# Identity products on TensorE beside a decode kernel's attention: the last kept unit and the twelve V's of a row's chain

## The chip, the cores and the metric

The kernel runs on one core of one Trainium2 chip. The metric is the device time of one execution in microseconds. The engines are named as in the profile: PE (TensorE's matmuls), PEld (its weight loads), DVE (VectorE), ACT (ScalarE), POOL (GpSimd) and SP (SyncE, which issues nearly all transfers).

## The reference

Two layers of attention over a long cache, each followed by a small MLP, run one after the other on the same row vector `x`; both use the same caches and weights. Eight batch rows, one token each, 16 query heads of 256 on 8 key/value heads, 4096 cached positions, model width 448, hidden width 1792.

```python
def _A_ref(x, k_cache, v_cache, wq, wo):          # x (8, 1, 448); caches (8, 8, 4096, 256), bf16
    q = (x @ wq).reshape(B, 1, 16, 256).transpose(0, 2, 1, 3)
    k, v = (jnp.repeat(c, 2, axis=1) for c in (k_cache, v_cache))
    p = softmax(einsum("bhqd,bhkd->bhqk", q, k) * 256 ** -0.5)
    o = einsum("bhqk,bhkd->bhqd", p, v)
    return o.transpose(0, 2, 1, 3).reshape(B, 1, 4096) @ wo

x = x + _A_ref(_layernorm(x), ...)
x = x + _B_ref(_layernorm(x), ...)
x = x + _A_ref(_layernorm(x), ...)
x = x + _B_ref(_layernorm(x), ...)
```

With one token per row the shifts in `_B_ref` push the mixing branch out of the window, so it comes to `x + gelu(layernorm(x) @ w3) @ w4`. The caches are 268 MB; the kernel reads them nearly twice, once for each layer, except for the parts that it keeps on the chip.

## The kernel before

**Units.** The work is cut into units (pass, row, gp): the pass is the first or second attention layer, gp is one of four pairs of key/value heads. A unit has four K chunks and four V chunks of 1 MB (128 partitions by 4096 bf16). `items` is the static order of all chunks; one loop walks over it (L1320 to the end of `layers_unshifted`), and each turn ends with `emit_loads`, which puts as many transfers into SP's queue as there are free places. There are 17 places of 1 MB in SBUF (`NC`, `places_t`).

**Kept units.** For each row the pairs `keep = [2, 3]` are loaded once: 14 of their 16 chunks stay in places from the first pass to the row's second pass, and two more are put away in PSUM banks (`away`, `part_words`, `inner_words`). So for each row the order is: the units of gp 2 and 3 in the first pass, with other units among them (`first_kept`); then the V's of the units that went ahead, which need the few places that are left; then gp 3 and gp 2 in the second pass from the kept places, which frees these for the loads of what follows.

**The chain.** When the V's of the last kept unit (0, row, gp 3) are done, the row's first attention layer is complete, and everything up to its second query can be worked out: the output projection, the MLP with its norms, and the projection of the new query (`chain`: `kept_half`, `mlp`, `project_q`; then `give_q`, which spreads the query with L439 on PE and L445 on DVE). This is a Python generator; `step` runs it from one `yield` to the next. Its pieces are put between the V's of three other units: twelve V chunks, each loaded as two halves (`halved`, L975). These twelve are `narrow`. For them `pv` (L1133) takes its 16 matmuls as two times eight and calls `between` in the middle, so that a piece of the chain can run after each half; the first of the twelve (`begins`) has no `between`. Ten of the twelve stand ahead of the row's second pass, two among its first scores.

**What PE runs.** `scores` (L1065) multiplies 8-column weights from the query with K, 256 columns at a time, in four column groups of the array; `pv` (L1133) does the same with the probabilities and V. `transpose_p` (L1116) turns the probabilities into `misc`, ACT copies them to `psv` (L1123). `wide` (L201) is the chain's product for one row: 128x128 weights and a vector that is read 32 times over, so 32 columns. In fp32 stand the sum of the norm (L290), the softmax sums (L562) and the scaling of a finished output (L630).

**Shared PSUM.** `misc` is one PSUM bank. Columns 0 to 127 belong to `transpose_p`; the chain's small results lie in the others, and DVE and ACT read them. PE runs its instructions in the order of the program, and a matmul into `misc` waits until the reads that the program holds it against are done.

**Queues.** All transfers of K, V and weights stand in SP's one queue, in the order of `items`. A K of the second pass's new units is loaded as a pair of 2 MB (L958) when two adjacent places are free; the halves of a `narrow` V (L975) when the half before has been multiplied out of its place.

The few lines that the edit touches in the loop are these (the condition of `between` and what follows `pv`):

```python
                pv(
                    o_now, slot, c, gp, ring_of[it],
                    (lambda: step(idx, True)) if it in narrow and it not in begins else None,
                    rest_t if halfway(it) else None,
                    it in fresh,
                )
                if ps == 0 and inside(it):
                    away(inner_words(slot))
```

Of the kernel before, what the change touches and what calls it, by code (L numbers as in the profile page):

```python
# [40 lines left out]
def layers_unshifted(  # L41
# [156 lines left out]
    def wide(out, w, x, start, stop):  # L198

        wide_done[0] += 1  # L200
        nc.tensor.matmul(  # L201
            bass.AP(out.tensor, out.offset, [out.ap[0], (1, WIDE)]),
            w,
            x.to_broadcast([128, WIDE]),
            start=start,
            stop=stop,
            skip_group_check=True,
        )

    def xbs(nb):  # L210
        return xb[1] if nb == 1 else xb[Bn][:, :, :nb]
# [913 lines left out]
    def pv(o_ps, v, a, gp, r, between, v2=None, fresh=False):  # L1125

        g = 2 * gp + a // 2
        for y in range(16):
            if y == 8 and between is not None:
                between()  # L1130
            q = y % 4
            at = 128 * r + 8 * (4 * q + y // 4) + 6 - 2 * (g % 4)
            nc.tensor.matmul(  # L1133
                o_ps[32 * q : 32 * q + 8, :],
                ptz[:, at : at + 8],
                v[:, y * Dh : (y + 1) * Dh]
                if v2 is None or y < PR
                else v2[:, (y - PR) * Dh : (y - PR + 1) * Dh],
                start=fresh and y < 4,
                stop=(y >= 12),  # L1140
                skip_group_check=True,
            )
# [177 lines left out]
    for idx, it in enumerate(items):  # L1320
# [80 lines left out]
        elif kv == 0:  # L1401
            if (ps, b) not in state:
                if ps == 1:
                    while (1, b) not in state:
                        step(10 * len(items), True, ("chain",))
                else:
                    state[0, b] = {}
            st = state[ps, b]
            who = q_key(ps, b, gp)
            if who not in q_of:  # L1410
                give_q(who)
            qbd = qbds[q_of.index(who)]
            if "z" not in st:
                z_t = chn.tile([128, 2, GP], FP32, tag="zall", bufs=8)
                st["z"] = z_t
                if final:
                    st["y"] = store[2][:, 0 : 4 * (Bn - MID)].rearrange("p (f b) -> p f b", f=4)
                    oc = store[3][:, 0 : 2 * Hq].rearrange("p (j h) -> p j h", j=2)
            if not kept_now:
                transpose_k(slot, late(it) and c % 2 == 0)  # L1420
            if c == 3 and q_begun:
                run(q_begun.pop())
            if not alone:
                step(idx)
            x = c - c % 2
            scored = not paired(n, c) or c % 2 == int(late(it))
            turn = turn_p if scored and p_of and n not in p_of else None
            if not paired(n, c):
                scores(p, c, qbd, gp, between=turn)
            elif scored:  # L1430
                two = [
                    where[(b, gp), (0, k)] if kept_now else where[n, 0, k] for k in (x, x + 1)
                ]
                if abs(two[1] - two[0]) == 1:
                    scores(two[0], x, qbd, gp, also=two[1], between=turn)
                else:
                    scores(two[0], x, qbd, gp, between=turn)
                    scores(two[1], x + 1, qbd, gp)
            if c == 1:
                p_n = work.tile([128, 4, 32, 4], BF16, tag="p_sb", bufs=1)  # L1440
                p_of[n] = p_n
            if c == 2:
                q_ahead(idx)
            if c % 2 == 1:
                exps(p_of[n], st["z"], gp, c // 2)
                if kept_now and c == 3:
                    alone.clear()
        else:
            st = state[ps, b]
            if ps == 1 and (halfway(it) or inside(it)):  # L1450
                while moves and any(w.offset == v.offset for _, w in moves for _, v in (part_words if halfway(it) else inner_words)(slot)):
                    move()
            if it in narrow and it[2] == 0 and not alone and any(e["kind"] == "chain" for e in gens):
                alone.append(n)
            if n in p_of:
                turn_p()
            spread_p(it)
            if it in v_next:
                spread_p(v_next[it])
            if final and gp in free and c == 1:  # L1460
                rz_gp = run(z_cols(st["z"], [gp]))
            if it not in narrow:
                step(idx)
            if final and gp in free:
                pv_cols(oc, slot, c, gp, psv[slot_of[n]])
                if c % 2 == 1:

                    u = c // 2
                    scale_o(oc, rz_gp, gp, u, OT2[:, :, :, b])
                    h0 = 8 * gp + 4 * u  # L1470
                    while any(e["kind"] == "last" for e in gens):
                        step(10 * len(items))
                    run(
                        add_cols(
                            st["y"],
                            lambda i: OT2[:, i % 2, i // 2, MID:],
                            lambda i, at: wo_of(i, at, end_wo),
                            range(h0, h0 + 4),
                            4,
                            open=(claim(st), gp == free[-1] and u == 1),  # L1480
                        )
                    )
            else:
                g8 = gp // 2
                alone_now = (ps, b) in split and gp in free
                if it == v_first[n] and ("o", g8) not in st:
                    while not free_o:
                        if not locked and not out_sb and waiting and waiting[0]["done"]():
                            empty(waiting[0])
                            clear(waiting.pop(0))  # L1490
                        else:
                            step(10 * len(items))
                    st["o", g8] = free_o.pop(0)
                    fresh.add(it)
                if it == v_first[n]:
                    o_of[n] = st["o", g8]
                o_now = o_of[n]
                kept_2 = (ps, gp) == (0, keep[0])
                if it == v_first[n] and (
                    alone_now or kept_2 or pairs_done.get((ps, b), 0) % 2 == 1  # L1500
                ):
                    done = pairs_done.get((ps, b), 0) + 1

                    def ready(k=(ps, b), done=done):
                        return pairs_done.get(k, 0) >= done

                    if ps == 0 and done == 4:
                        add_gen("chain", chain(b, st, ready), main=True)
                    elif kept_2:
                        rec = {"ps": st.pop(("o", 1))}  # L1510
                        add_gen("chain", kept_half(b, st, gp, ready, rec, 4))
                    elif ps == 1 and done == 2:
                        add_gen("chain" if final else "last", first_last(b, st, ready))
                    else:
                        rec = {"ps": st.pop(("o", 0)), "done": ready}
                        waiting.append(rec)
                        gps = [gp] if alone_now else free
                        if ps == 0:
                            add_gen("chain", first_half(b, st, gps, ready, rec))
                        else:  # L1520
                            add_gen("last", last(b, st, gps, ready, rec))
                pv(
                    o_now,
                    slot,
                    c,
                    gp,
                    ring_of[it],
                    (lambda: step(idx, True)) if it in narrow and it not in begins else None,
                    rest_t if halfway(it) else None,
                    it in fresh,  # L1530
                )
                if ps == 0 and inside(it):
                    away(inner_words(slot))
                if ps == 0 and halfway(it):
                    away(part_words(slot))
            if it == v_last[n]:
                pairs_done[ps, b] = pairs_done.get((ps, b), 0) + 1
                free_slots.append(slot_of.pop(n))
# [367 lines left out]
```

## Time and profile before

| | |
|---|---|
| median of 3 runs | 1033.46 us (1033.12 to 1033.53) |
| the profiled execution | 1034.17 us, of it the span 1032.5 us |
| instructions | 28801; PE 12708 matmuls and as many weight loads |
| busy | PE 658.4 us (64%), PEld 416.9 (40%), DVE 585.8 (57%), ACT 213.1 (21%), POOL 35.3 (3%) |
| granted TensorE clock, mean | 0.618 |
| transfers | 421.54 MB, mean 408 GB/s |
| matmuls, mean and count | L1133 382 ns x3808; L1065 384 ns x3456 with 256 columns, 274 ns x1280 with 128; L201 181 to 190 ns x2016; fp32 318 to 361 ns |

The span is the time from the first to the last instruction; the profiled execution's own time has a little more around it. The granted clock is the share of TensorE's pulses that its throttle let through. In the timeline a matmul's length holds its way through the array too, so that matmuls overlap: the pace is read from the distance of their starts. "idle before <-releaser" is the time that the engine sat idle and what ended it. The chain of work that ended last goes to 55% through transfers, to 20% through PE and to 18% through DVE.

### The profile page before, as it was taken

The numbers are of one execution on the slowest core, as the hardware profiler recorded it, in microseconds if no ns is written. First come the engines' busy times: TensorE is split into PE (matmuls) and PEld (weight loads), VectorE is DVE, ScalarE is ACT, GpSimd is POOL, SyncE is SP. The second block draws the span as 40 slices with busy tenths as digits, with TensorE's granted clock in tenths as the row PEclk, the third lists the DMA queues.
The fourth block names the chain that finished last, engine by engine and source line by source line (L and its number), as shares of the span: only waits on it lengthen the run. The fifth ranks groups of instructions, "written<-read, shape, count | busy, mean of one in ns | idle before, by whom it ended". The sixth has DMA issues, their size and how long they took to land.

```text
span 1032.5 us, 28801 instructions
## 1 busy us (share of the span) xinstructions
PE 658.4 (64%) x12708; PEld 416.9 (40%) x12708; DVE 585.8 (57%) x1213; ACT 213.1 (21%) x689; POOL 35.3 (3%) x138
## 2 busy tenths in 40 slices
PE   2153545876578658765775687557765775677675
PEld 2032323453245335532553355334533453345444
DVE  6345576259615961696159615971596159625672
ACT  1010111141204121412141204120412141204020
POOL 0000000000000000000000000000000000000000
PEclk9965555565656565755665657566656565667655
DMA  9999999999999999999999999999999999999994
GB/s 374 411 428 421 422 425 417 401 423 425 412 399 425 425 412 400 417 424 414 400 420 426 414 394 421 424 415 404 417 422 411 404 416 427 414 396 411 419 418 183
DMA packets 68016, 421.54 MB, mean 408 GB/s; under 512 B 7080, under 2 KB 11952, under 8 KB 42288
## 3 DMA queue, kind: packets, MB, share of 16 engines
q1 hardware_dynamic: 67840, 419.66, 99.0%
q8 instruction: 100, 1.64, 0.6%
q14 instruction: 28, 0.23, 0.1%
q10 hardware_dynamic: 48, 0.01, 0.0%
HBM read 419.63 MB, written 0.01 MB: 406 GB/s over the span
## 4 chain that ended last, share of the span: by engine, by line
DMA 55%; PE 20%; DVE 18%; issue 3%; ACT 2%; SPq 1%; POOL 0%; DVEq 0%; ACTq 0%
DMA places<-in_A_v_cache_dram 37%; DMA places<-in_A_k_cache_dram 17%; DVE places L1050 14%; PE sc L1065 8%; PE o L1133 5%; PE misc L630 2%; PE misc L201 2%; DMA w_sb<-in_B_w_dram 1%; DVE qbd L445 1%; ACT p_n L1074 1%; SPq L220 1%; DVE store L1096 1%; PE misc L562 1%; PE misc L483 0%; PE misc L1116 0%
## 5 line engine op out<-in xcount | busy, mean ns | idle before, releaser
L1050 DVE STREAM_TRANSPOSE places<-places 128x512 uint32<-128x512 uint32 (+2 forms) x384 | 443.9, 1212 | 43.9 <-DMA places<-in_A_k_cache_dram 43.6
L1133 PE MATMUL o<-places,ptw 128*8 128x256 bf16 x3808 | 246.7, 382 | 142.1 <-DMA places<-in_A_v_cache_dram 113.1
L1065 PE MATMUL sc<-places,qbd 128*8 128x256 bf16 (+1 forms) x4736 | 234.7, 354 | 147.7 <-DVE places L1050 145.8
L1065 PEld LDWEIGHTS <-qbd 128*8 128x8 bf16 x4736 | 122.5, 105 | 214.7 <-DVE places L1050 124.1
L1133 PEld LDWEIGHTS <-ptw 128*8 128x8 bf16 x3968 | 103.3, 102 | 208.8 <-issue 131.0
L1074 ACT ACTIVATE p_n<-sc 128x256 bf16<-128x256 f32 x128 | 95.5, 746 | 328.4 <-PE sc L1065 326.3
L1315 ACT COPY ptw<-psv 128x32 bf16<-128x32 bf16 x248 | 52.6, 227 | 179.5 <-PE o L1133 177.9
L445 DVE CAST qbd<-misc 32x16 bf16<-32x16 f32 (+1 forms) x184 | 30.8, 167 | 63.8 <-PE misc L439 61.9
L630 PE MATMUL misc<-R_t,o_t 128*128 128x4 f32 (+1 forms) x212 | 45.6, 322 | 27.3 <-DVE qbd L445 11.0
L630 PEld LDWEIGHTS misc<-R_t,o_t 128*128 128x128 f32 x212 | 41.4, 272 | 44.0 <-issue 17.2
L1123 ACT CAST psv<-misc 128x128 bf16<-128x128 f32 x64 | 17.0, 266 | 194.6 <-PE misc L1116 191.6
L565 DVE RECIPROCAL rz<-misc 128x4 f32<-128x4 f32 (+1 forms) x55 | 9.5, 172 | 82.8 <-PE misc L562 37.6
L1101 ACT COPY places<-store 128x1024 bf16<-128x1024 bf16 x40 | 40.2, 1027 | 10.5 <-PE o L1133 10.1
L562 PE MATMUL misc<-zm,few 128*128 128x4 f32 (+1 forms) x110 | 28.0, 325 | 18.9 <-DVE zm L554 16.5
L570 POOL TENSOR_TENSOR seen<-seen,rz 128x4 f32<-128x4 f32 (+1 forms) x55 | 11.0, 200 | 840.2 <-DVE rz L565 840.2
L562 PEld LDWEIGHTS misc<-zm,few 128*128 128x128 f32 x110 | 23.2, 262 | 35.0 <-DVE zm L554 23.3
L201 PEld LDWEIGHTS <-w_sb 128*128 128x128 bf16 x896 | 27.3, 104 | 16.1 <-issue 16.1
L1074 ACT ACTIVATION_READ_ACCUMULATOR p_n<-sc 128x1 f32 x128 | 33.8, 264 | 0.0
L584 ACT COPY o_t<-o 128x256 f32<-128x256 f32 x53 | 19.8, 373 | 58.9 <-PE o L1133 58.9
L1096 DVE TENSOR_SCALAR store<-places 128x512 uint32<-128x512 uint32 x40 | 24.8, 673 | 0.0
L634 DVE CAST qT<-misc 128x8 bf16<-128x8 f32 (+1 forms) x37 | 7.2, 196 | 28.8 <-PE misc L630 20.8
L1116 PEld LDWEIGHTS <-p_n 128*128 128x128 bf16 x256 | 11.5, 104 | 29.6 <-issue 18.5
(165 smaller groups left out, 393.1 us busy)
## 6 DMA issues: line engine op xcount, KB each, us to landing
places<-in_A_k_cache_dram SPq DMA_DIRECT2D x79, 2048.0 KB, 15.3
places<-in_A_v_cache_dram SPq DMA_DIRECT2D x193, 512.0 KB, 7.2
places<-in_A_v_cache_dram SPq DMA_DIRECT2D x87, 1024.0 KB, 19.2
places<-in_A_k_cache_dram SPq DMA_DIRECT2D x34, 1024.0 KB, 12.0
rest<-in_A_v_cache_dram SPq DMA_DIRECT2D x8, 640.0 KB, 16.7
places<-in_A_wq_dram SPq DMA_DIRECT2D x5, 768.0 KB, 12.7
places<-in_A_v_cache_dram SPq DMA_DIRECT2D x8, 384.0 KB, 16.3
wo_sb<-in_A_wo_dram SPq DMA_DIRECT2D x1, 2688.0 KB, 19.0
```

The lines of the kernel that those rows point to most:

```text
L201: nc.tensor.matmul(bass.AP(out.tensor, out.offset, [out.ap[0], (1, WIDE)]), w, x.to_broadcast([128, WIDE]), start=start, stop=stop, skip_g ...
L445: nc.vector.tensor_copy(qbd[32 * a : 32 * a + 32, :, g0 : g0 + ng, a, :], qs.rearrange("p e (f g u h) -> p (e f) u g h", f=2, u=2, h=2)[:, ...
L562: nc.tensor.matmul(z_ps, ones, zm[:], start=True, stop=True)
L584: nc.scalar.copy(o_t[:], rec["ps"])
L630: nc.tensor.matmul(ot_ps[:, j], o_sb[:].rearrange("p (i j) -> p j i", j=2)[:, j], R, start=True, stop=True)
L1050: nc.vector.transpose(w, w)
L1065: nc.tensor.matmul(sc[32 * k : 32 * k + 8, 128 * (x % 2) : 128 * (x % 2 + nx)], qbd[:, ep, gp % 2].rearrange("p a h -> p (a h)"), v, start ...
L1074: nc.scalar.activation(p_sb[:, :, :, 2 * u : 2 * u + 2].rearrange("p t i x -> p x t i"), sc[:, 0:256].rearrange("p (x t i) -> p x t i", x= ...
L1096: nc.vector.tensor_single_scalar(kept_words.bitcast(U32), words.bitcast(U32), 0, op=ALU.bitwise_or)
L1101: nc.scalar.copy(words, kept_words.bitcast(BF16))
L1133: nc.tensor.matmul(o_ps[32 * q : 32 * q + 8, :], ptz[:, at : at + 8], v[:, y * Dh : (y + 1) * Dh] if v2 is None or y < PR else v2[:, (y - ...
L1315: nc.scalar.copy(ptw[:, ring_of[it], :, 6:8], psv[slot_of[it[0]]][:, it[2]])
```

## The change

A function `fill(n)` issues n matmuls of the bf16 identity (128x128, as weights and as moving operand, 128 columns) into columns 0 to 127 of `misc`. Nobody reads what they write: `transpose_p` overwrites it. They are issued at four spots: after each K chunk and after each V chunk of the last kept unit of the first pass (ten each time), and in the middle and at the end of each `narrow` V (three each time; in the middle only where `between` is given).

```diff
+    def fill(n):
+
+        for _ in range(n):
+            nc.tensor.matmul(misc[:, 0:128], identb[:], identb[:], start=True, stop=True)
...
         for y in range(16):
             if y == 8 and between is not None:
+                fill(3)
                 between()
...
                     scores(two[0], x, qbd, gp, between=turn)
                     scores(two[1], x + 1, qbd, gp)
+            if (ps, gp) == (0, keep[1]):
+                fill(10)
             if c == 1:
...
                     rest_t if halfway(it) else None,
                     it in fresh,
                 )
+                if it in narrow:
+                    fill(3)
+                elif (ps, gp) == (0, keep[1]):
+                    fill(10)
                 if ps == 0 and inside(it):
```

On PE this adds 1192 matmuls and 1192 weight loads: in each of the eight rows 80 for the kept unit and 69 for the twelve V's. The order of all other instructions is as before on every engine. Eleven of the added matmuls in a row, the last row one fewer, wait for DVE or ACT to have read `misc`.

## The prediction

> **What bounds the kernel now.** I read the page's slices first, then stretches of one row's chain, then the order of instructions on PE inside them.
>
> ```profile
> PE   2153545876578658765775687557765775677675
> DVE  6345576259615961696159615971596159625672
> PEclk9965555565656565755665657566656565667655
> DMA  9999999999999999999999999999999999999994
> GB/s 374 411 428 421 422 425 417 401 423 425 412 399 425 425 412 400 417 424 414 400 420 426 414 394 421 424 415 404 417 422 411 404 416 427 414 396 411 419 418 183
> ```
>
> The DMA engines are busy from end to end: 421.5 MB at some 410 GB/s are the span of 1032.5 us. What can still be won are the dips to about 400 GB/s, one per batch row (eight, every fourth slice). In those slices PE is at its busiest (7 or 8 tenths) and DVE at its idlest: these are the chains. The granted clock stays near half there.
>
> ```profile
> 595.00:604.00 9.00, 8.10 (x149) 4.96 (x149) 1.95 (x12) 0.66 (x3) 0.70 (x1) 0.50 0.97 362
> 604.00:618.00 14.00, 10.72 (x218) 6.50 (x221) 3.21 (x18) 1.47 (x7) 0.55 (x1) 0.50 1.03 413
> 606.40:609.80 3.40, 3.31 (x73) 2.22 (x69) 0.66 (x4) 0.22 (x1) 0.00 (x0) 0.50 1.03 418
> 616.60:620.00 3.40, 2.72 (x52) 1.63 (x48) 0.00 (x0) 0.18 (x1) 0.00 (x0) 0.50 1.04 408
> 620.00:623.40 3.40, 2.21 (x58) 1.47 (x53) 0.98 (x6) 1.33 (x5) 0.00 (x0) 0.99 1.05 413
> ```
>
> Columns: stretch and its length, busy time of PE, PEld, DVE, ACT, POOL, then clock, DMA share, GB/s. One row's chain begins badly (362 GB/s for 9 us) and then runs at 413. Against 412 the eight beginnings lose 0.54, 0.49, 0.13, 0.26, 1.09, 0.21, 0.02 and 0.81 us (stretches of 5 to 9 us at 380, 383, 401, 394, 362, 395, 410, 345), and the eight starts of the second pass 0.29, 0.34, 0.54, 0.39, 0.05, 0.36, 0.20 and 0.60 us. Together 6.3 us (two of the stretches overlap a little): no more can be won.
>
> The third and fourth lines show what moves the clock. PE is busy for 3.31 of 3.40 us and the clock stays at half; it is busy for 2.72 us and the next stretch has the full clock. The records of the clock change only in steps of 3.413 us, that is 4096 columns at half clock (below). I counted the columns that the matmuls stream in each step, an 8-wide one (L1065, L1133) as a quarter, for four of them run abreast: 606.4 has 0.65 of 4096, 616.6 has 0.75. Of the half-clock steps from 50 us on, all 31 with over 0.74 are followed by a full one, 5 of 10 between 0.70 and 0.74, none of 190 below. A full step is kept by 17 of 17 over 0.70 and by 1 of 38 below.
>
> **The change part by part.** It adds 1192 matmuls of 128x128 by 128 columns and as many weight loads to PE and nothing to other engines: per row 8 bursts of ten in the unit gp 3, and 23 bursts of three in the twelve V's.
>
> *Price of one.* The trace has no such matmul. Its matmuls with 32 columns at L201 start 27 ns apart at half clock, 25 at full; an 8-wide one with 256 columns has its share of four abreast in 53 and 27 ns. So 128 columns take 107 ns at half clock (4 x 27), and at full between 53 (the same columns at twice the rate) and 100 (4 x 25, were those bound by columns). I take 53, for the columns of L1133 do halve: three cost 0.32 or 0.16 us, ten 1.07 or 0.53. The Trainium skill (TensorE: Matmul & The Clock Gate, Back-to-back issue gap) gives about 81 ns a matmul for a sustained stream of weight loads and matmuls of 128 columns; by that three cost 0.24 us and the sums below for the full clock rise by half. A burst between two V halves also changes weights twice where none did before: a half (8 matmuls, 0.43 us) has L201 0.53 us after it, and L201 x20 (0.54) is followed 0.74 us on, so 0.10 and 0.20 us; beside an L201 step nothing is added.
>
> *The tens.* Four bursts stand beside the unit's K chunks, four beside its V's; their places stay kept, so no transfer waits for them. Before 582.36 PE idles 2.46 us (row 5), enough for two bursts at half clock; 1.14 and 1.47 us before the last two V's take one each. Cost 0; without that cover, 8.5 us a row. They add 0.31 of a step each: 582.5 to 585.9 goes from 0.47 to 0.78, and the chain then begins at full clock. Only the burst after the last scores meets a gap (0.84 us) shorter than itself at half clock, 0.2 us, which the wait of 1.14 us takes up.
>
> *The threes, along the chain.* A step of the clock spans 2.7 V halves at 1.27 us. A half is 512 columns, a burst 384, L201 512 to 1024: with them 0.92 or more, without a product step 0.59. So the chain's products run at full clock, its bare halves not always. What that is worth:
>
> ```profile
> 605.43 0.60 PE L1133 MATMUL o<-places,ptw 128*8 128x256 bf16 x8 [0.81 <-DMA places<-in_A_v_cache_dram]
> 606.84 0.60 PE L1133 MATMUL o<-places,ptw 128*8 128x256 bf16 x8
> 608.28 0.60 PE L1133 MATMUL o<-places,ptw 128*8 128x256 bf16 x8
> ...
> 710.77 0.39 PE L1133 MATMUL o<-places,ptw 128*8 128x256 bf16 x8
> 711.10 0.86 PE L201 MATMUL misc<-HT_t,w_sb 128*128 128x32 bf16 x28
> 712.05 0.39 PE L1133 MATMUL o<-places,ptw 128*8 128x256 bf16 x8
> ```
>
> The same step (half a V and 28 products of L201) takes 1.41 and 1.44 us at half clock and 1.28 at full. The clock gives 0.15 us and the burst takes 0.16: PE's pace in these steps is what it was. Only the fp32 steps gain: four matmuls of L630 start 217 ns apart at half and 125 at full (0.37 us), two of L562 0.2, two pairs of L290 0.4; about 1 us a row less 0.16 for each burst among them, 0.5 us, most of it early in the chain, where the transfers are late. The beginnings lose 3.55 us in all; 0.5 a row but never more than what is lost gives 2.6 us as an upper end, and 0 the lower, since the transfers after that are paced by PE's equal steps. I take 1.4.
>
> *The start of the second pass.*
>
> ```profile
> 721.61 1.93 PE L1065 MATMUL sc<-places,qbd 128*8 128x256 bf16 x32
> 723.32 1.33 PE L1133 MATMUL o<-places,ptw 128*8 128x256 bf16 x16
> 724.43 1.76 PE L1065 MATMUL sc<-places,qbd 128*8 128x256 bf16 x32
> ...
> 513.50 1.11 PE L1065 MATMUL sc<-places,qbd 128*8 128x256 bf16 x32
> 514.53 0.39 PE L1133 MATMUL o<-places,ptw 128*8 128x256 bf16 x8
> 515.79 0.39 PE L1133 MATMUL o<-places,ptw 128*8 128x256 bf16 x8 [0.87 <-DMA places<-in_A_v_cache_dram]
> ```
>
> Here SP waits for these scores to free a pair of places for a K of 2 MB. At full clock they take 1.03 us in place of 1.71, yet the two rows that have it lose 0.29 and 0.39 us, the six others 0.35 on average: the loss hardly hangs on it. A burst of three now stands before the scores (0.16 + 0.30, or 0.32 + 0.30 at half clock), two more in the V behind them. Before the scores lie four bare halves (717.5 to 721.6), 0.59 of a step each, so I expect the full clock in half of the rows: two newly so (-0.68 + 0.46 each), the two that have it (+0.46 each), four at half (+0.6 each). Sum +2.9 us if each delay is lost in full, and 0 if the queue hides it; I take a third, as the loss followed the pace so little: +1.0.
>
> *Waits.* Ten bursts a row wait for DVE to have read misc. The longest stands behind L439: four casts of 0.17 us at L445, some 0.9 us against the 0.43 us of a half; behind it queue the next V half and SP's load for its place. It falls where PE waits 0.69 us for the V anyway: 0. Without that cover 0.5 us a row.
>
> *Fetching.* The instruction queues move 1.87 MB for 28801 instructions, 65 B each; 2384 more are 0.155 MB, at 408 GB/s +0.4 us.
>
> Sum: -1.4 + 1.0 + 0.4 = 0.0 us. The profiled execution took 1034.17 us (span 1032.5 and 1.7 around it), 0.7 above the median of 1033.46; the sum is a difference, so I put it on the median: 1033.5.
>
> **The rivals.** *Faster:* the full clock lets PE get ahead, and what the transfers lose shrinks in both places. For it: all eight beginnings lie at a clock of 0.50 to 0.54. Against: 604 to 618 at half clock moves 413 GB/s, 914 to 928 at 0.85 only 412. Two thirds of 6.3 less the fetching: -3.8, 1029.7. It holds if steps with 28 products fall to 1.3 us with their bursts.
>
> *Slower:* the bursts at the start of the second pass cost more than the clock gives. Place: the burst before the first scores and the two in the V after them. At half clock these are 3 x (0.32 + 0.30) = 1.9 us before the second K pair comes free, at full 3 x 0.46 less the 1.4 that two scores gain, about 0. It decides if the step before the scores falls below 0.70 in four rows or more and the loss is one for one, less the 0.8 that PE waits for V's there (0.87 at 515.79): 1.1 us x 4 or 5 = +5, 1038.5. For it: the queue holds only V halves there and each late place shows as a dip.
>
> *The clock is not moved:* products of identities may not count. Then each of some nine halves from 594.5 to 605.4, where PE waits for nothing, grows by 0.32: 2.9 us a row, +23, 1056. Against: L201, whose 32 columns are one column repeated, counts in full in the steps above. The Trainium skill (same page, Part 4: PE-mode transpose) says that transposes by TensorE do not count as busy in the way of other matmuls. The products here are plain matmuls with an identity; no run so far shows how those count.
>
> **How the numbers follow.** Forecast 0.45, faster 0.27, slower 0.24, clock not moved 0.04. A change under 0.2% (2.1 us) cannot be told from none here. So faster 0.27, same 0.45, slower 0.28. The range goes from 1028.5 (most of the 6.3 us) to 1038.5 (the second rival); the forecast's own is 1031.4 (no delay at the second pass, 2.6 won less 0.4) to 1036 (nothing won, 2.9 lost less what the queue hides).
>
> **What would show it.** A granted clock of 0.85 or more over each chain against 0.50 to 0.85, and steps with 28 products at 1.4 us in spite of it: right. Steps at 1.25 us, or chain beginnings at 405 GB/s: the faster rival. First scores of the second pass over 0.4 us later behind the last V half, at clock 0.5, with deeper dips: the slower one. The product at 80 ns or more at full clock, or long waits of the identity products for DVE, would make the sum wrong.

## The result and the profile after

The changed kernel takes 1037.9 us (median of 9 runs, 1035.99 to 1040.3), the kernel before 1033.46 in the same session (9 runs, 1032.83 to 1034.43). The ratio is 1.0040, with a 95% interval of 1.0031 to 1.0048: slower by 0.4%, about twice what counts as a difference here. The profiled execution took 1038.37 us with a span of 1036.6, against 1034.17 and 1032.5. Ratios in this document stand with their 95% intervals and are not quotients of the medians.

These are the slices of the changed kernel's page (40 equal parts of the span), the ones that were shown of before:

```profile
PE   2154547785677668766864788678867775786775
DVE  6345576259626961695269525882596259624572
PEclk9976557986897598766976886579758985886655
DMA  9999999999999999999999999999999999999994
GB/s 375 411 428 423 421 424 415 388 426 424 413 400 419 425 413 385 423 422 415 394 422 425 415 379 410 423 416 398 426 424 415 392 408 426 414 394 416 417 420 190
```

The clock row rose as intended: the mean over the run is 0.748 (0.618 before), and over the eight chains 0.94 (0.59 before; each chain taken from 2 us before its seventh V half is issued to the issue of its last one). But the dips of the transfers are deeper: 388, 385, 379 and 392 GB/s stand where 401, 400, 394 and 404 stood.

The instruction queue moved 1.80 MB in place of 1.64, and 421.70 MB in all in place of 421.54. So the extra time isn't extra data.

The added products are two groups of the page (line, engine, operation, count, busy us, mean ns, and the idle time before them with what ended it). L201 is the chain's product as before; lines behind it have moved on by 5 to 6: L213 is the added product, L1139 was L1133, L1070 was L1065, L635 was L630, L567 was L562.

```profile
L213 PE MATMUL misc<-identb 128*128 128x128 bf16 x1192 | 121.5, 240 | 6.5 <-DVE qbd L450 6.5
L213 PEld LDWEIGHTS <-identb 128*128 128x128 bf16 x1192 | 78.5, 106 | 67.0 <-issue 66.9
```

To see where the transfers lose, I measured, for each row, the time that they lose against 412 GB/s from the issue of the seventh V half to that of the last (the chain) and in the 14 us behind it (the start of the second pass). The chains lose 9.57 us in all, 4.47 before; the second pass's starts 2.02, 2.91 before. The sum went from 7.4 to 11.6, by 4.2 us, and the spans of the two profiled executions differ by 4.1. So in these two executions the loss lies in the chains, and not where the second pass starts.

Row 5 in stretches of the changed kernel (us, busy time of PE, PEld, DVE, ACT, POOL, then clock, DMA share, GB/s):

```profile
597.10:606.10 9.00, 6.66 (x152) 4.98 (x152) 1.95 (x11) 0.66 (x3) 0.87 (x3) 1.00 0.97 340
606.10:620.10 14.00, 11.71 (x252) 7.83 (x244) 3.20 (x18) 1.47 (x7) 0.55 (x1) 0.75 1.03 408
606.30:609.70 3.40, 3.14 (x58) 2.08 (x55) 0.69 (x4) 0.32 (x2) 0.00 (x0) 0.50 1.03 422
609.70:613.10 3.40, 3.34 (x85) 2.33 (x82) 0.93 (x6) 0.33 (x2) 0.00 (x0) 1.00 1.03 417
```

The beginning runs at the full clock and moves 340 GB/s; before, it ran at half clock and moved 362. PE is busy for 6.66 of 9 us where it was busy for 8.10. Then the clock falls to half for one step of 3.4 us in the midst of the chain. That happens in six of the eight rows (in row 5 the clock falls once more at 616.55, for two steps); the two rows without it (2 and 7) lose 0.56 and 0.89 us, the six others 0.87 to 1.79.

The timeline of row 3 shows what such a step costs (start, length, engine, line, tiles, count, and in brackets PE's idle time before it):

```profile
395.11 0.60 PE L1139 MATMUL o<-places,ptw 128*8 128x256 bf16 x8
395.64 0.50 PE L213 MATMUL misc<-identb 128*128 128x128 bf16 x3
395.93 0.76 PE L201 MATMUL misc<-xb,w_sb 128*128 128x32 bf16 x20
396.62 0.60 PE L1139 MATMUL o<-places,ptw 128*8 128x256 bf16 x8
...
400.54 0.39 PE L1139 MATMUL o<-places,ptw 128*8 128x256 bf16 x8 [0.26 <-DMA places<-in_A_v_cache_dram]
400.86 0.34 PE L213 MATMUL misc<-identb 128*128 128x128 bf16 x3
401.04 0.86 PE L201 MATMUL misc<-HT_t,w_sb 128*128 128x32 bf16 x28
401.83 0.39 PE L1139 MATMUL o<-places,ptw 128*8 128x256 bf16 x8
```

The first of these two steps in the kernel before, also at half clock:

```profile
393.21 0.60 PE L1133 MATMUL o<-places,ptw 128*8 128x256 bf16 x8
393.74 0.73 PE L201 MATMUL misc<-xb,w_sb 128*128 128x32 bf16 x20
394.48 0.60 PE L1133 MATMUL o<-places,ptw 128*8 128x256 bf16 x8
```

At half clock, half a V with the burst and 20 products of L201 takes 1.51 us; before it took 1.27, the pace at which halves arrive. At full clock half a V with the burst and 28 products takes 1.29.

### The profile page after: what moved, and what is told of

The parts are those of the page before. It is cut to its first block, busy times and chain, and to the rows that moved or that the text cites. A ratio compares the mean times of both kernels' runs of the same rounds, so it can differ in the third digit from the quotient of the medians.

```text
span 1036.6 us, 31187 instructions
## 1 busy us (share of the span) xinstructions
PE 693.1 (67%) x13900; PEld 461.6 (45%) x13900; DVE 585.5 (56%) x1213; ACT 212.5 (21%) x689; POOL 35.3 (3%) x138
## 2 busy tenths in 40 slices
DMA packets 68026, 421.70 MB, mean 407 GB/s; under 512 B 7080, under 2 KB 11952, under 8 KB 42288
## 4 chain that ended last, share of the span: by engine, by line
DMA 55%; PE 20%; DVE 18%; issue 3%; ACT 2%; SPq 2%; POOL 0%; DVEq 0%; ACTq 0%
DMA places<-in_A_v_cache_dram 38%; DMA places<-in_A_k_cache_dram 15%; DVE places L1055 14%; PE sc L1070 6%; PE o L1139 6%; PE misc L213 3%; PE misc L635 2%; DMA w_sb<-in_B_w_dram 1%; PE misc L201 1%; ACT p_n L1079 1%; DMA places<-in_A_wq_dram 1%; SPq L225 1%; DVE store L1101 1%; DVE qbd L450 1%; PE misc L488 1%
## 5 line engine op out<-in xcount | busy, mean ns | idle before, releaser
L1070 PE MATMUL sc<-places,qbd 128*8 128x256 bf16 (+1 forms) x4736 | 222.0, 336 | 134.7 <-DVE places L1055 132.3
L1139 PE MATMUL o<-places,ptw 128*8 128x256 bf16 x3808 | 211.4, 334 | 124.5 <-DMA places<-in_A_v_cache_dram 97.7
L1070 PEld LDWEIGHTS <-qbd 128*8 128x8 bf16 x4736 | 114.5, 100 | 196.3 <-DVE places L1055 105.2
L1139 PEld LDWEIGHTS <-ptw 128*8 128x8 bf16 x3968 | 92.5, 96 | 170.6 <-issue 101.2
L1079 ACT ACTIVATE p_n<-sc 128x256 bf16<-128x256 f32 x128 | 95.5, 746 | 332.7 <-PE sc L1070 330.1
L213 PE MATMUL misc<-identb 128*128 128x128 bf16 x1192 | 121.5, 240 | 6.5 <-DVE qbd L450 6.5
L213 PEld LDWEIGHTS <-identb 128*128 128x128 bf16 x1192 | 78.5, 106 | 67.0 <-issue 66.9
L570 DVE RECIPROCAL rz<-misc 128x4 f32<-128x4 f32 (+1 forms) x55 | 9.5, 172 | 95.8 <-ACT ptw L1321 58.1
L635 PE MATMUL misc<-R_t,o_t 128*128 128x4 f32 (+1 forms) x212 | 41.3, 301 | 32.0 <-DVE qbd L450 11.4
L635 PEld LDWEIGHTS misc<-R_t,o_t 128*128 128x128 f32 x212 | 37.0, 245 | 46.9 <-ACT o_t L589 14.8
L1079 ACT ACTIVATION_READ_ACCUMULATOR p_n<-sc 128x1 f32 x128 | 33.9, 265 | 0.0
L567 PE MATMUL misc<-zm,few 128*128 128x4 f32 (+1 forms) x110 | 24.8, 296 | 13.1 <-DVE zm L559 10.2
L567 PEld LDWEIGHTS misc<-zm,few 128*128 128x128 f32 x110 | 20.5, 233 | 23.5 <-DVE zm L559 16.3
L201 PEld LDWEIGHTS <-w_sb 128*128 128x128 bf16 x896 | 28.1, 98 | 1.2 <-issue 1.0
```

The source lines that it names most:

```text
L201: nc.tensor.matmul(bass.AP(out.tensor, out.offset, [out.ap[0], (1, WIDE)]), w, x.to_broadcast([128, WIDE]), start=start, stop=stop, skip_g ...
L213: nc.tensor.matmul(misc[:, 0:128], identb[:], identb[:], start=True, stop=True)
L567: nc.tensor.matmul(z_ps, ones, zm[:], start=True, stop=True)
L635: nc.tensor.matmul(ot_ps[:, j], o_sb[:].rearrange("p (i j) -> p j i", j=2)[:, j], R, start=True, stop=True)
L1070: nc.tensor.matmul(sc[32 * k : 32 * k + 8, 128 * (x % 2) : 128 * (x % 2 + nx)], qbd[:, ep, gp % 2].rearrange("p a h -> p (a h)"), v, start ...
L1079: nc.scalar.activation(p_sb[:, :, :, 2 * u : 2 * u + 2].rearrange("p t i x -> p x t i"), sc[:, 0:256].rearrange("p (x t i) -> p x t i", x= ...
```

## The experiments

All were timed in five rounds against the kernel before (medians 1033.23 to 1033.41). The first four take the change apart, the next four test the clock, the last four the shared bank and the length of the bursts. Four of the twelve (the threes alone, the tens beside K only, and the two kernels of sixes behind bare steps and threes behind product steps that keep the tens) came out above every range that was expected of them, so none of the explanations tried foresaw their loss.

**Tens alone** (the bursts of three left out):

```diff
-                fill(3)
                 between()
...
-                if it in narrow:
-                    fill(3)
-                elif (ps, gp) == (0, keep[1]):
+                if (ps, gp) == (0, keep[1]):
                     fill(10)
```

> Only the bursts of ten beside the last kept unit's chunks; the bursts of three are left out. Half-clock theory (the threes cost where the clock falls to half for one step inside the chain): 1033 to 1034 us, chain stretches lose no more than before (4.5 us in all against 412 GB/s). Late-start theory (the tens beside the unit's V's push the chain's first half back): 1036 to 1038 us, most of the 4.4 us stays. Cast theory (in two rows DVE's cast L639 waits for a burst that stands beside a K chunk): 1034.5 to 1036 us, the 3.4 us wait in the fifth row stays.

Measured: 1035.51 us (1034.72 to 1039.98), ratio 1.0027 [1.0017, 1.0037]. The tens are not free: they cost some 2.8 us by the ratio. The median lies in the range that the casts would give; the later burst below speaks against these. This is row 3 of this kernel (its V's are at L1138):

```profile
387.11 0.39 PE L1138 MATMUL o<-places,ptw 128*8 128x256 bf16 x8 [0.78 <-DMA places<-in_A_v_cache_dram]
387.44 0.63 PE L635 MATMUL misc<-R_t,o_t 128*128 128x4 f32 x4
388.39 0.39 PE L1138 MATMUL o<-places,ptw 128*8 128x256 bf16 x8 [0.32 <-DMA places<-in_A_v_cache_dram]
388.72 0.61 PE L201 MATMUL misc<-OT,wo_sb 128*128 128x32 bf16 x16
389.65 0.60 PE L1138 MATMUL o<-places,ptw 128*8 128x256 bf16 x8 [0.32 <-DMA places<-in_A_v_cache_dram]
```

The chain begins at full clock, and PE is ahead: it waits for V at each of these halves. Here what the clock gives turns into waits for transfers, which come no sooner.

**Threes alone** (the tens left out):

```diff
-            if (ps, gp) == (0, keep[1]):
-                fill(10)
...
-                elif (ps, gp) == (0, keep[1]):
-                    fill(10)
```

> Only the bursts of three beside the twelve V's; the tens are left out. Half-clock theory: 1037 to 1041 us, as much as the whole change or more, for the chain now starts at half clock. Late-start theory: 1033 to 1034.5 us. Cast theory: 1034.5 to 1036.5 us, no wait of L639 for the products.

Measured: 1044.4 us (1041.4 to 1044.87), ratio 1.0095 [1.0082, 1.0108]. The parts don't add up: the threes cost 9.8 us alone, but only 1.3 on top of the tens (1.0040 against 1.0027).

**Tens beside K only, and the threes** (the four tens beside the unit's V's left out):

```diff
-                elif (ps, gp) == (0, keep[1]):
-                    fill(10)
                 if ps == 0 and inside(it):
```

> As the changed kernel without the tens beside the kept unit's four V's; those beside its K chunks and all threes stay. Half-clock theory: 1037 to 1040 us. Late-start theory: 1034 to 1035 us, the first half of a chain starts 1 to 2.5 us sooner after the unit's first V. Cast theory: 1037 to 1038 us, the wait stays.

Measured: 1042.94 us (1039.39 to 1050.43), ratio 1.0105 [1.0079, 1.0132]. So it is the tens beside the V's, just ahead of the chain, that make the threes cheap.

**A later burst** (two output casts, L639 in rows 5 and 8, wait for an identity product, the longer one 3.4 us; here the second K's ten is issued with the third's, and those waits are gone):

```diff
-            if (ps, gp) == (0, keep[1]):
-                fill(10)
+            if (ps, gp) == (0, keep[1]) and c != 1:
+                fill(20 if c == 2 else 10)
```

> The same products as in the changed kernel, but the ten beside the unit's second K chunk are issued with those of its third, so that they stand behind the cast L639 in the program. Half-clock and late-start theories: 1037 to 1039 us, as the changed kernel. Cast theory: 1035 to 1036.5 us, the fifth row's scores of the unit's third and fourth K chunk no longer come 3 to 5 us later than before, and no wait of L639 for L213.

Measured: 1037.72 us (1036.43 to 1039.3), ratio 1.0045 [1.0032, 1.0058], as the change. So the casts are not the cause of what the change costs.

**Sixes in place of threes**, to keep the clock full in every step:

```diff
-                fill(3)
+                fill(6)
                 between()
...
                 if it in narrow:
-                    fill(3)
+                    fill(6)
```

> Bursts of six in place of three at every spot of the twelve V's, tens as in the changed kernel. Half-clock theory (bursts cost where the chain's products meet the half clock; a bare half with six streams 1280 of the 1520 columns that its 1.27 us hold, so the clock no longer falls): clock 1.0 through every chain and 1034 to 1037 us, less than the changed kernel. Pace theory (each product costs PE's time whatever the clock): 138 more bursts' worth of 0.16 us a row are lost in part, 1042 us or more.

Measured: 1043.27 us (1041.6 to 1044.03), ratio 1.0092 [1.0078, 1.0107]. The clock over the chains rose to 0.96, and the kernel became slower still. So the steps at half clock are not the whole story: doing away with most of them by more products costs more than it gives. (The sixes add 69 products a row, which is 23 bursts of three and not 138.)

**Sixes behind bare steps alone** (those without L201, behind the chain's step, the tens kept), **threes behind product steps alone** (tens kept), and **the sixes behind bare steps without tens**. The core of the first; the second has `> done` and `fill(3)` there, the third is the first with the tens left out as in the threes alone:

```diff
-                fill(3)
+                done = wide_done[0]
                 between()
+                if wide_done[0] == done:
+                    fill(6)
```

> Six products behind a chain step that issues no L201 products, none behind one that does; tens as in the changed kernel. Half-clock theory: the clock stays full through the chain and the product steps carry no burst: 1032 to 1035 us. Pace theory: 1036 to 1038 us, for there are more products (1312) than in the changed kernel (1192).

> Three products only behind a chain step that issues L201 products, none in bare halves; tens as in the changed kernel. Half-clock theory: the clock falls in the norm's bare halves and the products that follow meet it with their bursts: 1035 to 1039 us. Pace theory: 1035 us, half of the threes' cost is gone.

> As the six-in-bare-halves kernel without the tens. Half-clock theory: the chain starts at half clock, but its product steps have no burst to carry there, so 1033 to 1036 us against 1044.4 for threes everywhere without tens. Pace theory: 672 products against 552, so 1044 us or more.

Measured: 1041.95 us (1040.4 to 1045.22), ratio 1.0089 [1.0075, 1.0103]; 1041.8 us (1040.36 to 1046.75), 1.0091 [1.0075, 1.0107]; 1044.24 us (1040.35 to 1048.9), 1.0097 [1.0082, 1.0112]. No placing is cheaper than the change's own, and none is better than before. These three kernels differ from the change in a second way: their bursts stand behind the chain's step and not ahead of it, and so behind matmuls whose results DVE still has to read from `misc`. PE waits for DVE at the bursts for 15.3, 8.7 and 15.3 us, of which 13.0, 8.7 and 13.0 lie between the issues of the seventh and the last V half; in the change its bursts wait for 6.5 us, none of it there. So these runs don't tell by themselves which steps should carry the bursts.

**Threes into another bank.** The products write into `misc`, the bank from which DVE and ACT read the chain's results. Here the threes go to `sc`, which the chain doesn't read; once with the tens, once without:

```diff
-    def fill(n):
+    def fill(n, to=misc):
...
-            nc.tensor.matmul(misc[:, 0:128], identb[:], identb[:], start=True, stop=True)
+            nc.tensor.matmul(to[:, 0:128], identb[:], identb[:], start=True, stop=True)
...
-                fill(3)
+                fill(3, sc)
```

> The changed kernel with the bursts of three written to the scores' bank sc (columns 0 to 127) in place of misc, the tens as they are. Shared-bank theory (a read of a chain result in misc that stands behind a burst in the program waits for that burst, which stands behind a V half; first of all the reciprocal of the softmax sum, 1.8 us late in the third row): 1032 to 1035 us, the reciprocal follows L567 within 0.2 us and the products of L635 follow their V half without a wait of 0.54 us. Half-clock theory: 1036 to 1039 us, PE carries the same products at the same places.

> The bursts of three alone, written to sc; without tens. Against 1044.4 us with the same bursts in misc. Shared-bank theory: 1033 to 1037 us. Half-clock theory: 1042 to 1046 us.

Measured: with tens 1038.26 us (1037.0 to 1039.58), ratio 1.0044 [1.0030, 1.0057]; without 1037.24 us (1035.26 to 1038.45), ratio 1.0039 [1.0026, 1.0053]. Without tens the other bank is worth 5.8 us (1.0095 to 1.0039); with tens it is worth nothing that can be measured. The exchange isn't free of waits: in `sc` two bursts a row, behind the chain and among the first scores of the second pass, wait for ACT, which reads the scores there (L1079). This is the burst's row among PE's waits in the changed kernel, then the two of the threes in `sc` with tens (total us, times, longest us):

```profile
PE misc L213 <- DVE qbd L450: 6.5, 14, 0.6
PE sc L213 <- ACT ptw L1321: 4.5, 8, 0.6
PE sc L213 <- ACT p_n L1079: 4.4, 8, 0.6
```

A part of the 5.8 us is seen at the start of a chain. Row 5 of before, then of the threes alone, then of the threes alone in `sc`, on PE:

```profile
593.95 0.60 PE L1133 MATMUL o<-places,ptw 128*8 128x256 bf16 x8 [0.46 <-DMA places<-in_A_v_cache_dram]
594.48 1.01 PE L630 MATMUL misc<-R_t,o_t 128*128 128x4 f32 x4
595.42 0.60 PE L1133 MATMUL o<-places,ptw 128*8 128x256 bf16 x8
```

```profile
599.92 0.60 PE L1139 MATMUL o<-places,ptw 128*8 128x256 bf16 x8 [0.45 <-DMA places<-in_A_v_cache_dram]
600.46 0.50 PE L213 MATMUL misc<-identb 128*128 128x128 bf16 x3
601.50 1.01 PE L635 MATMUL misc<-R_t,o_t 128*128 128x4 f32 x4 [0.54 <-DVE R_t L618]
602.44 0.60 PE L1139 MATMUL o<-places,ptw 128*8 128x256 bf16 x8
```

```profile
593.99 0.60 PE L1139 MATMUL o<-places,ptw 128*8 128x256 bf16 x8 [0.45 <-DMA places<-in_A_v_cache_dram]
594.52 0.50 PE L213 MATMUL sc<-identb 128*128 128x128 bf16 x3
594.82 0.96 PE L635 MATMUL misc<-R_t,o_t 128*128 128x4 f32 x4
595.71 0.60 PE L1139 MATMUL o<-places,ptw 128*8 128x256 bf16 x8
```

From half to half it is 1.47, 2.52 and 1.72 us. The burst alone is 0.3 of that; the other 0.7 is PE waiting for DVE's result behind it (0.54 of it in brackets). On DVE the first operation of that step is the reciprocal of the softmax sums (L570). In the threes alone, and then in the threes alone in `sc`:

```profile
601.06 0.18 DVE L570 RECIPROCAL rz<-misc 128x4 f32<-128x4 f32 x1 [8.81 <-PE misc L213]
```

```profile
593.09 0.18 DVE L570 RECIPROCAL rz<-misc 128x4 f32<-128x4 f32 x1 [6.59 <-ACT ptw L1321]
```

With `sc` it runs during the first half V, 0.7 us after the sums started (592.40). With `misc` it waits until the burst behind the second half is through, though it reads other columns of the bank. That order is the program's: in this row of the threes alone the semaphore that L570 waits for is raised by the last product of the burst, and the second matmul of the sums raises none; with the burst in `sc` that second matmul raises it.

**No burst behind the first of the twelve V's**, which removes just that wait, with tens:

```diff
-                if it in narrow:
+                if it in narrow and it not in begins:
                     fill(3)
```

> The changed kernel without the one burst of three behind the first of the twelve V's, the burst that the reciprocal waits for (8 x 3 products fewer of 1192). Shared-bank theory: 1034.5 to 1037 us, for the chain's beginning loses up to 0.9 us a row less. Half-clock theory: 1037 to 1038.5 us, no change that can be seen.

Measured: 1038.35 us (1037.22 to 1039.92), ratio 1.0048 [1.0034, 1.0062]. The reciprocal starts 0.44 us after the sums in every row, as in the tens alone, where the change has 1.3 to 2.2. With tens, this wait costs nothing that can be measured.

**Threes alone, 32 columns wide**, in `misc`: the same instructions in the same order as in the threes alone, a quarter of the columns.

```diff
-            nc.tensor.matmul(misc[:, 0:128], identb[:], identb[:], start=True, stop=True)
+            nc.tensor.matmul(misc[:, 0:32], identb[:], identb[:, 0:32], start=True, stop=True)
```

> Threes alone into misc, as in the run of threes alone (1044.4 us), but with 32 columns each in place of 128: the same instructions, the same order at the shared bank, a quarter of the columns, 27 ns a product by L201. If the order at the bank makes the 7 us between threes into misc (1044.4) and threes into sc (1037.2), only the columns' part of the rest goes: 1040 to 1044, and waits of DVE for the products stay near 63 us. If the time of the products makes the loss, a quarter is left of it: 1034 to 1036. The clock should stay near that of before (0.62), as the columns of three such products are 96 of 4096.

Measured: 1036.41 us (1033.76 to 1040.31, 11 runs), ratio 1.0033 [1.0021, 1.0044]. DVE's waits for the burst are still there:

```profile
DVE rz L570 <- PE misc L213: 56.3, 8, 7.6
```

(total us, times, longest us; 63.2, 8 and 8.8 in the threes alone. Most of each is time in which DVE sits idle there in any case: 6.59 us in the row of `sc` above.) So the order at the bank by itself isn't the 5.8 us, nor are the products' columns by themselves, as far as these two runs tell: it takes a long burst and readers that stand behind it. Either cure, another bank or short products, removes most of the loss; the expectation of the bank alone missed by 3.6 us, that of the products' time alone by 0.4.

**The beginnings side by side.** From the timelines I took, in each row, the time from the first half V behind the last kept unit's sums (L567) through nine halves, and how much of it PE waited for V. Means over the eight rows of one profiled execution each; the clock is that over the chains, and the ratio that of all runs. A single execution can lie away from its kernel's median: by 4.7 us for the sixes behind bare steps without tens (1048.9), by -2.0 for the threes in `sc` without tens (1035.26).

| kernel | clock | nine halves, us | of it waiting for V | without it | ratio |
|---|---|---|---|---|---|
| before | 0.59 | 11.35 | 1.54 | 9.81 | 1 |
| tens alone | 0.68 | 11.16 | 2.42 | 8.74 | 1.0027 |
| the change | 0.94 | 11.52 | 1.55 | 9.97 | 1.0040 |
| threes in `sc`, tens | 0.90 | 11.33 | 2.02 | 9.31 | 1.0044 |
| not behind the first V, tens | 0.90 | 12.03 | 2.52 | 9.51 | 1.0048 |
| sixes, tens | 0.96 | 11.88 | 0.94 | 10.94 | 1.0092 |
| 32 columns, no tens | 0.65 | 11.98 | 0.73 | 11.25 | 1.0033 |
| threes in `sc`, no tens | 0.79 | 11.81 | 0.88 | 10.93 | 1.0039 |
| later burst, tens | 0.90 | 11.95 | 1.31 | 10.64 | 1.0045 |
| sixes behind bare steps, tens | 0.91 | 11.14 | 1.71 | 9.43 | 1.0089 |
| threes behind product steps, tens | 0.75 | 12.74 | 1.75 | 10.99 | 1.0091 |
| sixes behind bare steps, no tens | 0.76 | 12.03 | 1.15 | 10.88 | 1.0097 |
| threes alone | 0.76 | 12.49 | 0.69 | 11.80 | 1.0095 |
| threes, tens beside K only | 0.80 | 12.52 | 0.76 | 11.76 | 1.0105 |

Two things are to be read from it. In the last two rows the beginnings, which start at half clock (0.50 to 0.73 granted over 12.5 us from the sums), are 1.14 and 1.17 us longer; eight times that is 9.1 and 9.4 us, close to their loss of 9.8 and 10.9. And in five of the kernels with tens PE needs about as much as before or less (8.74 to 9.97), but waits as long or longer for V (1.55 to 2.52): there the transfers come late though PE isn't slow in these halves. The table doesn't explain everything: the threes behind product steps are longer by 1.39 us, 11.1 in eight rows, more than their 9.4 us of loss, while the sixes (0.53 x 8 = 4.2 of 9.5 us) and the sixes behind bare steps with tens (shorter by 0.21 us, at 1.0089) lose most or all of theirs after these nine halves.

## Why the forecast of no change missed and the range held

The forecast was no change, 1033.5; the result is 4.4 us above it, inside the range up to 1038.5 and outside the forecast's own up to 1036. That the range held is luck: its upper end was worked out for delays where the second pass starts, and the transfers lose no more there than before.

*Right: the price and the clock.* An identity product starts 107 ns after the one before at half clock and 56 ns at full (107 and 53 were predicted). The Trainium skill's 81 ns a matmul (TensorE: Matmul & The Clock Gate, Back-to-back issue gap) is not the distance at either clock in these bursts of three and ten. The rule of columns held in the changed kernel: of the half-clock steps with over 0.74 of 4096 columns 43 of 44 are followed by a full one, of those below 0.70 none of 105; full steps were kept by 81 of 81 above 0.74 and by 2 of 45 below 0.70 (matmuls at the edge of a step shift these counts by a few). The products of identities count in full, so the rival by which they don't falls. What the Trainium skill says of transposes on the same page (Part 4: PE-mode transpose) doesn't carry over to a plain matmul with an identity.

*Right: fetching* (0.16 MB; the 0.4 us were not measured by themselves) and *the waits* as far as they are hidden. The prediction counted bursts that wait for readers and left out readers that wait for a burst: PE stands 0.54 us behind the first burst in each row. From the issue of the seventh V half to that of the last PE waits 5.1 us for DVE where it waited 0.4, and its bursts 6.5 us behind that. With the threes in `sc` and tens PE's waits for DVE in the chains are 0.4 us again, and the chains still lose 10.6 us. So with the tens these waits don't make the loss; without tens the bank that they come from is worth 5.8 us.

*Wrong: "The tens ... Cost 0".* Alone they cost 2.8 us [1.8 to 3.8]. The gaps on which I laid them are not there in each row: in row 3 the unit's first three V's had landed before PE came to them (they start at 380.09, 381.30 and 382.50, 1.2 us apart, with no wait for a transfer), so their tens stand in PE's way. But for the fourth, at 384.49, PE waits 0.71 us again. How the tens turn into transfers lost isn't shown.

*Wrong: the term of the chains' beginnings, "I take 1.4" of gain.* This is the term that failed, in sign: the chains lose 5.1 us more, of which the beginning's nine halves are (11.52 - 11.35) x 8 = 1.4. I argued that the transfers are late where PE is slow, so that a faster clock there would bring them back, and set 0 as the worst. The tens alone refute both: PE's need over nine halves (their time without the waits for V) fell from 9.81 to 8.74 us, twice the 0.5 us a row that I had put in, and the kernel became slower; 0.88 of the 1.07 us became waits for V.

*Wrong: "PE's pace in these steps is what it was".* It leant on 1.28 us as PE's need at full clock. That step was paced by the transfers: with the burst in it, it takes 1.29. At half clock the burst does lengthen the step (1.51 for 1.27), and half clock still falls on product steps in six rows, against the forecast that the chain's products run at full clock. The steps with 28 products at full clock came out at 1.29 us, between the 1.4 that was to show the forecast right and the 1.25 of the faster rival, and neither sign told the time.

*Wrong: the start of the second pass* was set at +1.0 and measured at -0.9 us (one profiled execution of each kernel).

*The rivals.* The slower one named 1038.5 and a dip behind the chain; the time came, the place didn't. Its idea that a burst delays the loads behind it fits the steps at half clock in the chain (1.51 us for 1.27), but no run shows that these steps make the loss. The faster one needed dips that a faster PE fills; the tens alone show that it didn't fill them.

*What stays open.* Seven quite different kernels (tens alone, the change, the later burst, the threes in `sc` with and without tens, none behind the first V, 32 columns) all lie at 1.0027 to 1.0048. The three with 552 or 640 added products lie at 1.0027 to 1.0039, the four with 1168 or 1192 at 1.0040 to 1.0048, and their intervals overlap. Whether one small cause that each added burst brings is behind them, or several, these runs don't tell. Why the kernels with bursts at fewer places (threes behind product steps, sixes behind bare ones) are slower than the change with all of them isn't shown either; their bursts wait for DVE inside the chains, which would fit, and no run takes these waits away. Nothing tried here is faster than the kernel before.

## What to carry to other kernels

Where transfers bound the kernel, ask of a filler product first whether PE has anything to gain: here the tens alone cut PE's need by 1.1 us over nine halves, and 0.9 of it became waits for V. Products that fill for the clock are work between two loads that wait for a free place, and their length counts at the clock that they meet: in the threes alone, 0.3 us at half clock between a result and its reader cost more than twice that. If filler must be, look at which reads the program orders behind it: another bank was worth 5.8 us without the tens and nothing with them. And remember that the parts of such an edit are not additive: 2.8 and 9.8 us apart, 4.1 together.

## What the runs showed of the hardware that wasn't expected

- An executed kernel with bursts varies more from run to run: 1035.99 to 1040.3 and 1033.76 to 1040.31 where the kernel before has 1032.8 to 1034.9. That the 3.4 us steps of the clock fall differently on the chains each time would do this; no run shows it.
- Columns streamed, not time busy, moved the clock again: a half-clock step of the changed kernel with PE busy for 3.14 of 3.40 us (606.3) is followed by the full clock, one of the kernel before with 3.31 isn't. By the sum of columns, 148 of the changed kernel's 149 half-clock steps outside the band from 0.70 to 0.74 come out right, give or take a few by where matmuls at the edge of a step are counted.
